# Diagonal score blocks on 32-row steps, a reversed key order for odd heads, and a new order of all queues in a two-kind attention kernel

## The chip, the cores and the metric

The kernel runs on one core of a Trainium2 chip. The metric is the device time of one execution in microseconds; the time before is the median of three runs, 480.24 us (479.35 to 480.51). A core has five instruction queues that run beside each other: TensorE (PE, with its weight loads shown as PEld), VectorE (DVE), ScalarE (ACT), GpSimd (POOL) and SyncE (SP, which issues most DMAs). Each queue runs in the order in which it was written; between queues only semaphores order the work.

## The reference

Four layers with a residual each, in the order A, B, A, B, on 2048 tokens of width 512 with 32 heads of 16. A is attention in four segments of 512 tokens with a running memory, B is linear attention with a softmax feature map. Both begin with a layer norm. Cut to what matters:

```python
# A, for segment s of 512 tokens
logits = einsum('bhqd,bhkd->bhqk', qs, ks) * 0.25 + mask     # mask: keys after the query are out
p = softmax(logits)
a_dot = einsum('bhqk,bhkd->bhqd', p, vs)
num, den = phi(qs) @ M, phi(qs) @ z + 1e-6                   # memory of the segments before
o = g * num / den + (1 - g) * a_dot
M, z = M + phi(ks)^T vs, z + sum(phi(ks))
# B, over all 2048 tokens
phi_k = [softmax(k w_phi), softmax(-k w_phi)];  phi_q likewise
o = phi_q @ (phi_k^T v) / (phi_q @ sum(phi_k) + 1e-6)
```

## The kernel before

**Stages.** `build` records about 3,100 operations for two layers; each layer is one A and one B. In A the core walks through four segments (`a_proj`, `a_att`, `a_state`, `a_mem`), and the key part of B (`b_keys`) for a segment's tokens and the query part (`b_queries`) are recorded between them. `b_out` of the first layer's chunks 1 to 3 is recorded among the second layer's A segments, so the second layer's attention has more PE work beside it.

**Scores.** `a_att` makes scores transposed: keys on the 128 partitions, queries along the row. A head has only 16 numbers, so a 32-row strip of PE holds two heads; the keys of the even head (`par` 0) and of the odd head (`par` 1) stand in two copies, each with zeros where the other head's rows are. Four strips `a` = 0 to 3 lie in the four 32-row groups of the array. One score operation `y` does strips 2y and 2y+1 into a pair of PSUM banks, 512 columns each; one ACT instruction then takes the exp of both banks at once (`128x1024`) into a tile PT. Where the order marks it, two score operations are issued interleaved, so that all four row groups work (a matmul list of 28 in place of 14).

**Diagonal blocks.** A unit with two diagonal blocks D and one full block S fills the 512 columns of a bank: 3 x 64 for each D and 128 for S. For one D, the even and the odd head share 192 columns of 128 rows: 64 columns hold the first 64 queries of both heads, over a stationary operand KP that has the first 64 keys of the even head in rows 0 to 63 and those of the odd head in rows 64 to 127; then 64 columns with the later 64 queries of each head. KP is copied together from K once per 128 tokens (L938 and L939), and the odd head's keys stand with their two halves of 64 swapped: `a_proj` makes a 64-column second copy of the normed input (`lo`, L907) so that a window of 128 columns over it reads the tokens in that order. The triangle is cut out after the exp by two kinds of masks: `mask.odd` (L1110) multiplies the odd heads' part by a 0/1 table `modd` into a tile D, in two instructions of 256 elements a row (either on DVE or on POOL), and `mask.even` (L1113), always on POOL, clears the even heads' part of PT in place with a select. The even mask waits for both odd masks of its tile, since they share columns. Then `pv` multiplies each 128 x 128 block of PT or D (as weights) by 17 columns of V.

**What sets the order.** Nothing is scheduled at build time. `replay` takes four tables: `ORDER` lists every operation by number (a number over 10000 is interleaved with the one before it; a negative one puts idle matmuls on the tile `warm` into PE's queue, L1431), `ENGINE` says which engine takes each operation that may run on several, `SLOTS` which buffer each tile gets, `AFTER` adds waits. All buffers, waits and queue positions follow from them.

Of the kernel before, what the change touches and what calls it, by code (L numbers as in the profile page):

```python
# [20 lines left out]
NG = 4  # L21
# [518 lines left out]
class Kernel:  # L540
# [299 lines left out]
    def xtiles(self, xnT):  # L840

        return xnT.ap if xnT.pool is self.p_xA else xnT.ap[:].rearrange("p t (d c) -> p t d c", d=4)
# [191 lines left out]
    def a_att(self, s, tss, seg, AM, starts, ends, done, by_pe=()):  # L1034
# [22 lines left out]
        for n, unit in enumerate(units):  # L1057
# [8 lines left out]
            if diag:  # L1066
                offs = [0, 4, 2]
# [408 lines left out]
```

## Time and profile before

The page of the profiled execution gives the span (first to last instruction), each engine's busy time, and where the chain of waits ran that ended last. Busy time of PE is modelled from pipelined matmuls and runs high.

| | before |
|---|---|
| median of three runs | 480.24 us |
| profiled execution, span | 479.8 us |
| instructions | 19249 |
| PE busy, by the trace | 464.4 us (97%), 8324 matmuls |
| ACT busy | 430.7 us (90%), 668 instructions |
| DVE busy | 428.1 us (89%), 1021 instructions |
| POOL busy | 261.0 us (54%), 420 instructions |
| first attention exp starts, last one ends | 12.8 us, 433.3 us |
| last exp of layer 0 ends, first of layer 1 starts | 203.4 us, 238.8 us |
| granted TensorE clock | 1.00 throughout |

The stages used below are read off the exps: 12.8 to 203.4 us is the attention of layer 0, 203.4 to 238.8 us the step between the layers, 238.8 to 433.3 us the attention of layer 1, and the rest is start and tail.

### The profile page before, as it was taken

The numbers are of one execution on the slowest core, as the hardware profiler recorded it, in microseconds if no ns is written. First come the engines' busy times: TensorE is split into PE (matmuls) and PEld (weight loads), VectorE is DVE, ScalarE is ACT, GpSimd is POOL, SyncE is SP. The second block draws the span as 40 slices with busy tenths as digits, with TensorE's granted clock in tenths as the row PEclk, the third lists the DMA queues.
The fourth block names the chain that finished last, engine by engine and source line by source line (L and its number), as shares of the span: only waits on it lengthen the run. The fifth ranks groups of instructions, "written<-read, shape, count | busy, mean of one in ns | idle before, by whom it ended". The sixth has DMA issues, their size and how long they took to land.

```text
span 479.8 us, 19249 instructions
## 1 busy us (share of the span) xinstructions
PE 464.4 (97%) x8324; PEld 320.1 (67%) x8324; DVE 428.1 (89%) x1021; ACT 430.7 (90%) x668; POOL 261.0 (54%) x420
## 2 busy tenths in 40 slices
PE   8999989999999999999999999999999999999997
PEld 7776667667856567557687666766865657665763
DVE  6999999989998988599999899999998879978785
ACT  3999999999999999986799899899999999999743
POOL 3577657646756576410246485784776578761100
PEclk9999999999999999999999999999999999999999
DMA  8978752225411232232257407236145112402376
GB/s 264 160 196 132 127 78 46 46 48 78 59 23 25 46 68 47 19 39 47 55 88 93 62 9 124 58 53 81 39 56 89 25 25 48 76 19 55 69 128 187
DMA packets 115091, 35.86 MB, mean 75 GB/s; under 512 B 106816, under 2 KB 115008, under 8 KB 115008
## 3 DMA queue, kind: packets, MB, share of 16 engines
q1 hardware_dynamic: 113184, 33.06, 39.9%
q10 hardware_dynamic: 1824, 1.58, 1.0%
q8 instruction: 65, 1.06, 0.9%
q14 instruction: 18, 0.15, 0.1%
HBM read 6.32 MB, written 2.10 MB: 18 GB/s over the span
## 4 chain that ended last, share of the span: by engine, by line
PE 40%; DVE 25%; ACT 22%; DMA 8%; POOL 3%; issue 1%; POOLq 0%; DVEq 0%
PE PS L520 38%; ACT PT L1104 16%; DVE stats L801 4%; DMA OT<-O 3%; ACT Ek L1200 3%; DVE xn L817 2%; DVE X L1165 2%; DMA EQ<-xn 2%; POOL PT L1113 2%; DVE Vt L1228 1%; DVE D L1110 1%; DMA xA<-xn 1%; DMA xB<-xn 1%; PE PS L1431 1%; DVE O L1139 1%
## 5 line engine op out<-in xcount | busy, mean ns | idle before, releaser
L1104 ACT ACTIVATE PT<-PS 128x1024 bf16<-128x1024 f32 x288 | 282.4, 1068 | 6.5 <-PE PS L520 5.6
L1110 POOL TENSOR_TENSOR D<-PT,modd 128x256 bf16<-128x256 bf16 x127 | 87.2, 697 | 41.7 <-ACT PT L1104 29.5
L1113 POOL TENSOR_SCALAR_AFFINE_SELECT PT<-PT 128x512 bf16<-128x512 bf16 x128 | 83.2, 658 | 48.1 <-DVE D L1110 43.3
L520 PEld LDWEIGHTS PS<-VT,PT 128*128 128x128 bf16 x2048 | 74.7, 96 | 18.7 <-POOL PT L1113 3.8
L520 PE MATMUL PS<-VT,PT 128*128 128x17 bf16 x2048 | 81.7, 171 | 1.5 <-POOL PT L1113 0.6
L520 PE MATMUL PS<-QT,K 32*128 32x64 bf16 (+2 forms) x2176 | 74.8, 213 | 1.1 <-ACT PT L1104 0.6
L520 PE MATMUL PS<-VT,D 128*128 128x17 bf16 x512 | 59.8, 170 | 0.0
L520 PEld LDWEIGHTS PS<-QT,K 32*128 32x128 bf16 x2176 | 40.4, 93 | 20.3 <-ACT PT L1104 10.0
L1110 DVE TENSOR_TENSOR D<-PT,modd 128x256 bf16<-128x256 bf16 x129 | 45.1, 364 | 2.1 <-ACT PT L1104 2.0
L520 PEld LDWEIGHTS PS<-VT,D 128*128 128x128 bf16 x512 | 43.2, 96 | 0.0
L1228 DVE TENSOR_TENSOR Vt<-PS,Zk 128x1024 bf16<-128x1024 f32 (+1 forms) x34 | 38.9, 1159 | 1.1 <-ACT Zk L1216 0.6
L801 DVE BATCH_NORM_STATS2 stats<-X 128x6 f32<-128x512 bf16 x56 | 37.6, 683 | 1.1 <-DMA X<-in_A_x_dram 0.7
L1200 ACT ACTIVATE Ek<-PS 128x512 bf16<-128x512 f32 x64 | 36.8, 648 | 1.6 <-PE PS L520 1.4
L1207 POOL TENSOR_TENSOR Vt<-Ek 128x512 f32<-128x512 bf16 x24 | 28.2, 1175 | 17.4 <-ACT Ek L1200 15.1
L520 PE MATMUL PS<-WA_k,xA 128*128 128x256 bf16 x256 | 36.6, 273 | 0.8 <-DVE xA L907 0.5
L1165 DVE TENSOR_TENSOR X<-X,PS 128x512 bf16<-128x512 bf16 x50 | 33.5, 678 | 4.3 <-PE PS L520 4.0
L1304 POOL COPY O<-rho 128x512 bf16<-128x512 bf16 x26 | 16.2, 642 | 38.7 <-DVE rho L1297 35.4
L520 PE MATMUL PS<-xA,WA_q 128*128 128x128 bf16 x512 | 36.4, 219 | 0.7 <-DMA xA<-xn 0.5
L520 PE MATMUL PS<-WA_v,xA 128*128 128x256 bf16 x256 | 36.3, 273 | 0.3 <-DMA xA<-xn 0.3
L520 PE MATMUL PS<-WA_o,OT 128*128 128x512 bf16 x128 | 32.1, 380 | 1.3 <-DMA OT<-O 0.7
L520 PEld LDWEIGHTS PS<-xA,WA_q 128*128 128x128 bf16 x512 | 30.0, 98 | 4.8 <-issue 1.0
L817 DVE TENSOR_SCALAR xn<-X,mv,rstd 128x512 bf16<-128x512 bf16 x64 | 28.6, 466 | 4.1 <-POOL rstd L813 1.7
(158 smaller groups left out, 983.5 us busy)
## 6 DMA issues: line engine op xcount, KB each, us to landing
X<-in_A_x_dram SPq DMA_DIRECT2D x3, 512.0 KB, 11.7
out_dram<-X SPq DMA_DIRECT2D x12, 128.0 KB, 1.8
EQ<-in_B_wqkv_dram SPq DMA_DIRECT2D x2, 512.0 KB, 4.9
OT<-O SPq DMA_TRANSPOSE x42, 3.2
WB_v<-in_B_wqkv_dram SPq DMA_DIRECT2D x1, 512.0 KB, 10.9
WA_o<-in_A_wo_dram SPq DMA_DIRECT2D x1, 512.0 KB, 4.1
WB_o<-in_B_wo_dram SPq DMA_DIRECT2D x1, 512.0 KB, 4.9
out_dram<-X ACTq DMA_DIRECT2D x4, 128.0 KB, 2.3
```

What stands on the lines that cost most here:

```text
L520: return e.matmul(o, l, r, start=st, stop=sp, tile_position=(basep(l), basep(o)))
L801: self.dve(lambda e, t=t, src=src: e.bn_stats(self.stats[:, t, :], src()), 0.603, [held() if held else R("X", t)], [R("stats", t)], name=" ...
L817: self.dve(lambda e, t=t, n=n, xn=xn: e.tensor_scalar(xn.ap[:, n], self.X[:, t, :], self.mv[:, t, 0:1], self.rstd[:, t:t + 1], op0=ALU.sub ...
L1104: self.act(lambda e, st=st, pt=pt: e.activation(pt.ap[:].rearrange("p b c -> p (b c)"), self.ps[:, st.slot[0] * 512:st.slot[0] * 512 + 102 ...
L1110: self.either(lambda e, d=d, k=k, pt=pt: e.tensor_tensor(d.ap[:, :, k, :].rearrange("p b (z c) -> p b z c", z=2), self.ends(pt.ap[:, :, 25 ...
L1113: self.pool(lambda e, q=quarters: e.affine_select(q(), q(), [[0, 4], [1, 128]], ALU.is_ge, 0.0, base=0, channel_multiplier=-1), 0.6, [pt() ...
L1139: self.dve(lambda e, r1=r1, view=view, nt=nt, g=g, o=o[ts]: e.tensor_tensor(o.ap[:, 0:nt, g, :].rearrange("p i (h d) -> p i h d", d=DH), v ...
L1165: self.dve(lambda e: e.tensor_tensor(X[:, t, :], X[:, t, :], self.bank(gen), ALU.add), 0.6, [R("X", t), gen()], [R("X", t)], name="resid")
L1200: self.act(lambda e, sgn=sgn, Ek=Ek, gen=gen: e.activation(Ek.ap[:, sgn, :], self.bank(gen), ACT.Exp, scale=1.0 - 2.0 * sgn), 512, [gen()] ...
L1207: self.pool(lambda e, Ek=Ek, sums=sums: e.tensor_tensor(sums(), *(Ek.ap[:].rearrange("p s (h j) -> p s h j", h=H)[:, :, :, 8 * k:8 * k + 8 ...
L1228: self.dve(lambda e, w=w, n=n, Vt=Vt, Zk=Zk, gen2=gen2: e.tensor_tensor(self.signed(Vt)[:, w, :, 0:16], self.bank(gen2).rearrange("p (h d) ...
L1304: P.add(("act", "pool"), {"act": lambda e, dst=dst, src=src: e.activation(dst(), src(), ACT.Copy), "pool": lambda e, dst=dst, src=src: e.t ...
```

## The change

A diagonal block takes 160 columns in place of 192, so a unit with two of them fills 448 of a bank's 512 columns and its exp runs over `128x896`. The odd head's keys now stand in fully reversed token order (key 127 - p in row p), so that the even head's triangle lies in the upper rows and the odd head's in the lower rows of shared columns. A block is made by five matmuls on each strip in place of three: even keys x queries 32 to 127 (96 columns); odd keys x queries 64 to 127 in reversed order (64 columns); odd keys, rows 64 to 127 only, x queries 32 to 63 (32 columns); odd keys, rows 96 to 127 only, x queries 0 to 31 (32 columns); even keys, rows 0 to 31 only, x queries 0 to 31 (32 columns). The last three write over parts that the masks would clear. KP and its copies are gone; `lo` now copies 128 reversed columns; for the tiles whose keys come straight from PSUM the odd copy is one instruction in place of two. `mask.odd` is one instruction over 512 elements a row that reads PT backwards: a multiplication on DVE or a select on POOL.

The two small odd blocks take their queries forwards, while the mask reads those columns backwards: for the first 64 queries of a diagonal tile the odd heads' scores are those of the query mirrored within its 32 columns. Amount and kind of work are the same as with the other direction.

```diff
-        self.p_xA = slots("xA", 2, [128, 4, 4, 192], BF16)
+        self.p_xA = slots("xA", 2, [128, 4, 4, 256], BF16)
-        self.p_KP = slots("KP", 4, [128, NG, 128], BF16)
...
+    def turn(self, a):
+        n = a.shape[-1]
+        return bass.AP(a.tensor, a.offset + n - 1, [list(x) for x in a.ap[:-1]] + [[-1, n]])
...
-            lo_d, lo_s = (lambda tt=tt: self.xcol(xnT, slice(None), tt, 128, 64)), (lambda tt=tt: self.xcol(xnT, slice(None), tt, 0, 64))
+            lo_d, lo_s = (lambda tt=tt: self.xcol(xnT, slice(None), tt, 128)), (lambda tt=tt: self.turn(self.xcol(xnT, slice(None), tt)))
...
-            op = P.add(("dve", "act", "pool"), {"dve": lambda e, d=kp_d, s=kp_s: e.tensor_copy(d(), s()), ...
-                       {"dve": 0.21, "act": 0.53, "pool": 0.58}, [K((0, tt)), K((1, tt)), K((1, tt, 1)), K(("both", tt))], [kp()], lat=0.08, name="kp")
...
+            cols = [(128, 0), (288, 160), (0, 320)] if diag else [(64 * off, 64 * off) for off in offs]
+            wide = 448 if diag else 512
...
-                        put(lambda a, g=g, i=i: both(a, g, i), item, i * 128, off, 64)
-                        for par in range(2):
-                            put(lambda a, par=par, g=g, i=i: strip(a, par, g, i), item, i * 128 + 64, 6 + off // 4 if par else off + 1, 64)
+                        keys = lambda par, lo, hi, g=g, i=i: lambda a: strip(a, par, g, i, lo, hi)
+                        put(keys(0, 0, 128), item, i * 128 + 32, x, 96, 64)
+                        put(keys(1, 0, 128), item, i * 128 + 64, x, 64, back=True)
+                        put(keys(1, 64, 128), item, i * 128 + 32, x, 32, 64, 64, 128)
+                        put(keys(1, 96, 128), item, i * 128, x, 32, 96, 96, 128)
+                        put(keys(0, 0, 32), item, i * 128, x, 32, 32, 0, 32)
...
-                    for k in range(2):
-                        self.either(lambda e, d=d, k=k, pt=pt: e.tensor_tensor(
-                            d.ap[:, :, k, :]..., self.ends(pt.ap[:, :, 256 * k:256 * k + 64], 384 - 192 * k), self.modd[:]..., ALU.mult), 0.21, 0.63, ..., name="mask.odd")
+                    op = P.add(("dve", "pool"), {"dve": lambda e, odd=odd, turned=turned: e.tensor_tensor(odd(), turned(), self.modd[:, None, :].to_broadcast([128, 4, 128]), ALU.mult),
+                                                 "pool": lambda e, odd=odd, turned=turned: e.affine_select(odd(), turned(), [[0, 4], [1, 128]], ALU.is_ge, 0.0, base=-127, channel_multiplier=1)},
+                               {"dve": 0.334, "pool": 0.59}, [pt(), pt("e"), R("modd")], [d()], lat=0.08, port=True, name="mask.odd")
```

All four tables are new; a line of `ORDER`, its first, was and is:

```diff
-    0, 20, 26, 1, 23, 21, 22, 2, 3, 24, 25, 28, 4, 5, 33, 81, 27, 6, 7, 82, 8, 9, 10, 11, 53, 16, 54, 18, 55, 60, 56, 17, 57, 12, 61, -401, 62, 63,
+    26, 0, 20, -323, 11, 2, 78, 8, 6, 4, 10, 5, 79, 21, 24, 1, 25, 27, 31, 30, 3, 22, 7, 14, 50, 9, 17, 51, 52, 32, 57, 13, 53, 18, 54, 58, 55, 59,
```

How many instructions of each kind there are, counted over the whole program (before, now): matmuls 8326 and 9230, among them idle ones on `warm` 144 and 24; exps over 1024 columns 288 and 160, over 896 columns 0 and 128; `mask.odd` on DVE 129 (256 elements a row) and 49 (512), on POOL 127 and 79; KP copies 32 and 0; stretches of score matmuls between other PE work 175 and 162, of which 85 and 76 hold a diagonal block. The stores of the result are split 12 on SP and 4 on ACT before, 8 and 8 now.

**First place: PE, the first interleaved pair of diagonal units (layer 0, segment 0).** Names: QT holds the queries, K the keys, KP the joined keys; the size is output rows x columns. Before:

```order
L520 MATMUL PS<-WA_v,xA0 128x256 x4
L1431 MATMUL PS<-warm 128x240 x2
L520 MATMUL PS<-QT0,KP0 128x64 x4
L520 MATMUL PS<-QT0,K0 128x64 x8
L520 MATMUL PS<-QT0,KP1 128x64 x4
L520 MATMUL PS<-QT0,K0 128x64 x8
L520 MATMUL PS<-QT0,K0 128x128 x4
```

and now, up to the first of the two diagonal blocks (the second follows with the same four rows, and then the 128 columns of the full block):

```order
L519 MATMUL PS<-WA_k,xA0 128x256 x4
L519 MATMUL PS<-QT1,K0 128x96 x4
L519 MATMUL PS<-QT1,K0 128x64 x4
L519 MATMUL PS<-QT1,K0 64x32 x4
L519 MATMUL PS<-QT1,K0 32x32 x8
```

The pair went from 28 to 44 matmuls, with outputs of 128, 64 and 32 rows one after the other, and the idle matmuls ahead of it are gone.

**Second place: POOL, the masks in layer 0.** PT holds exps, D the odd heads' masked part, `modd` the 0/1 table. Before:

```order
L1110 TENSOR_TENSOR D1<-PT4,modd 128x2x128
L1113 AFFINE_SELECT PT4<-PT4 128x4x128
L1110 TENSOR_TENSOR D2<-PT8,modd 128x2x128 x2
L1113 AFFINE_SELECT PT8<-PT8 128x4x128
L938 COPY KP2<-K1 128x2x4x64
```

and now:

```order
L1199 TENSOR_TENSOR Vt0<-Ek2 128x512
L1099 AFFINE_SELECT D2<-PT6 128x512
L1101 AFFINE_SELECT PT6<-PT6 128x4x128
L1099 AFFINE_SELECT D1<-PT8 128x512
L1101 AFFINE_SELECT PT8<-PT8 128x4x128
L1099 AFFINE_SELECT D3<-PT9 128x512
```

A tile's two odd masks became one select that stands just ahead of its even select on the same queue, and the KP copies between them are gone.

**Third place: PE at the start of segment 3 of layer 0.** Before:

```order
L520 MATMUL PS<-VT1,PT5 128x17
L520 MATMUL PS<-VT1,D2 128x17
L520 MATMUL PS<-QT1,K1 128x128 x16
L1431 MATMUL PS<-warm 128x240 x12
L520 MATMUL PS<-QT0,KP1 128x64 x4
L520 MATMUL PS<-QT0,K1 128x64 x8
```

and now:

```order
L519 MATMUL PS<-MSb1,PhiQ0 128x128 x8
L1423 MATMUL PS<-warm 128x240
L519 MATMUL PS<-QT2,K1 128x128 x2
L519 MATMUL PS<-QT1,K1 128x96 x2
L519 MATMUL PS<-QT2,K1 128x128 x2
L519 MATMUL PS<-QT1,K1 128x64 x2
L519 MATMUL PS<-QT2,K1 128x128 x2
L519 MATMUL PS<-QT1,K1 64x32 x2
L519 MATMUL PS<-QT2,K1 128x128 x2
L519 MATMUL PS<-QT1,K1 32x32 x4
```

The 12 idle matmuls that stood between two stretches of score work have gone, a plain unit is now interleaved with a diagonal one, and so 128-row, 64-row and 32-row outputs alternate.

More of the change, by code (lines that the diff above doesn't have):

```diff
@@ L713, in setup @@
         m = self.p_D.tile()
-        tri = lambda dst, src, base, step: pool(lambda e: e.affine_select(dst(), src(), [[step, 128]], ALU.is_ge, 0.0, base=base, channel_multiplier=1 if step == 0 else -1), 0.3, [m()], [m()])
-        m0, m1, m2 = (lambda: m.ap[:, 0, 0, :]), (lambda: m.ap[:, 0, 1, :]), (lambda: m.ap[:, 1, 0, :])
-        pool(lambda e: e.memset(m0(), 1.0), 0.2, (), [m()])
-        tri(m1, m0, 64, 1)
-        tri(m2, m1, -64, 0)
-        tri(m1, m0, -64, 1)
-        pool(lambda e: e.tensor_tensor(self.modd[:], m1(), m2(), ALU.add), 0.3, [m()], [R("modd")])
+        pool(lambda e: e.memset(m.ap[:, 0, 0, :], 1.0), 0.2, (), [m()])
+        pool(lambda e: e.affine_select(self.modd[:], m.ap[:, 0, 0, :], [[1, 128]], ALU.is_ge, 0.0, base=-127, channel_multiplier=1), 0.3, [m()], [R("modd")])
         for par in range(2):
@@ L894, in a_proj @@
         K, VT = self.p_K.tile(), self.p_VT.tile()
-        seg = dict(K=K, VT=VT, KP=[self.p_KP.tile() for _ in range(4)], QT=[self.p_QT.tile() for _ in range(2)])
+        seg = dict(K=K, VT=VT, QT=[self.p_QT.tile() for _ in range(2)])
         if s >= 1:
@@ L915, in a_proj @@
                 for par in range(2):
-                    for z in range(par + 1):
-                        cd = slice(tt * 128 + 64 * z, tt * 128 + (64 * z + 64 if par else 128))
-                        cs = slice(64 * (1 - z), 64 * (2 - z)) if par else slice(0, 128)
-                        dst = lambda par=par, cd=cd: K.ap[:, par, :, cd]
-                        src = lambda gen=gen, cs=cs: self.bank(gen).rearrange("p (g c) -> p g c", g=NG)[:, :, cs]
-                        P.add(("act", "dve"), {"act": lambda e, dst=dst, src=src, par=par: e.activation(dst(), src(), ACT.Copy, scale=self.even[:, par:par + 1]),
-                                               "dve": lambda e, dst=dst, src=src, par=par: e.tensor_scalar(dst(), src(), self.even[:, par:par + 1], None, op0=ALU.mult)},
-                              {"act": 0.36 if par else 0.57, "dve": 0.36 if par else 0.667}, [gen(), R("even", par)], [K((par, tt) if z == 0 else (par, tt, 1))], lat=0.1, name="kfm.copy")
+                    dst = lambda par=par, sl=sl: K.ap[:, par, :, sl]
+                    src = lambda gen=gen, par=par: (self.turn if par else lambda a: a)(self.bank(gen).rearrange("p (g c) -> p g c", g=NG))
+                    P.add(("act", "dve"), {"act": lambda e, dst=dst, src=src, par=par: e.activation(dst(), src(), ACT.Copy, scale=self.even[:, par:par + 1]),
+                                           "dve": lambda e, dst=dst, src=src, par=par: e.tensor_scalar(dst(), src(), self.even[:, par:par + 1], None, op0=ALU.mult)},
+                          {"act": 0.57, "dve": 0.667}, [gen(), R("even", par)], [K((par, tt))], lat=0.1, name="kfm.copy")
             else:
@@ L1075, in a_att @@
                     for c, i in enumerate(item[4]):
-                        where[item[1], item[2], item[3], i] = (pts, lambda d, b, x=(off + 2 * c) * 64: d[:, b, x:x + 128])
+                        where[item[1], item[2], item[3], i] = (pts, lambda d, b, x=(col[0] + 128 * c, wide + col[1] + 128 * c): self.flat(d)[:, x[b]:x[b] + 128])
             P.tag = (self.L, "att%d" % s)
@@ L1086, in f @@
                         def f(a=2 * y + b, b=b):
-                            x = st.slot[b] * 512 + c * 64
-                            return (self.ps[:, x:x + m], left(a), qt.ap[32 * a:32 * a + 32, item[1], q % 256:q % 256 + m], True, True)
+                            at = st.slot[b] * 512 + x[b] + dx
+                            qs = qt.ap[32 * a:32 * a + 32, item[1], q % 256:q % 256 + m]
+                            return (self.ps[lo:hi, at:at + m], left(a), self.turn(qs) if back else qs, True, True)
                         mms.append((f, m // 4))
-                for item, off in zip(unit, offs):
+                for item, x in zip(unit, cols):
                     g = item[1]
@@ L1093, in a_att @@
                         par, j, qs = item[2:]
-                        reads += [K((par, j)), K((par, j, 1)), K(("both", j))] + [QT[i // 2](i % 2) for i in qs]
-                        put(lambda a, par=par, g=g, j=j: strip(a, par, g, j), item, qs[0] * 128, off, 128 * len(qs))
+                        reads += [K((par, j)), K(("both", j))] + [QT[i // 2](i % 2) for i in qs]
+                        put(lambda a, par=par, g=g, j=j: strip(a, par, g, j), item, qs[0] * 128, x, 128 * len(qs))
                     else:
@@ L1102, in a_att @@
                 op = self.pe(mms, reads, [st()], pre=[pt], lat=0.23, cost=0.23, rows=y + 1, name="score")
                 op.place = (self.L, s, n)
[L1104 to L1105 removed]
+                self.act(lambda e, st=st, pt=pt, wide=wide: e.activation(
+                    self.flat(pt.ap)[:, 0:2 * wide].rearrange("p (b c) -> p b c", b=2), self.ps[:, st.slot[0] * 512:st.slot[0] * 512 + 1024].rearrange("p (b c) -> p b c", b=2)[:, :, 0:wide], ACT.Exp, scale=0.25), 2 * wide, [st()], [pt()], name="exp")
@@ L1106, in a_att @@
                 if diag:
                     d = ds[y]
-                    quarters = lambda pt=pt: pt.ap[:].rearrange("p b (k c) -> p (b k) c", k=2)[:, :, 0:128]
-                    for k in range(2):
-                        self.either(lambda e, d=d, k=k, pt=pt: e.tensor_tensor(
-                            d.ap[:, :, k, :].rearrange("p b (z c) -> p b z c", z=2), self.ends(pt.ap[:, :, 256 * k:256 * k + 64], 384 - 192 * k),
-                            self.modd[:].rearrange("p (z c) -> p z c", z=2)[:, None].to_broadcast([128, 2, 2, 64]), ALU.mult), 0.21, 0.63, [pt(), pt("e"), R("modd")], [d(k)], name="mask.odd")
+                    quarters = lambda pt=pt: self.every(self.flat(pt.ap)[:, 160:288], 160, 4)
@@ new lines, in a_att @@
+                    odd, turned = (lambda d=d: d.ap[:].rearrange("p b k c -> p (b k) c")), (lambda pt=pt: self.turn(self.every(self.flat(pt.ap)[:, 128:256], 160, 4)))
+                    op = P.add(("dve", "pool"), {"dve": lambda e, odd=odd, turned=turned: e.tensor_tensor(odd(), turned(), self.modd[:, None, :].to_broadcast([128, 4, 128]), ALU.mult),
+                                                 "pool": lambda e, odd=odd, turned=turned: e.affine_select(odd(), turned(), [[0, 4], [1, 128]], ALU.is_ge, 0.0, base=-127, channel_multiplier=1)},
+                               {"dve": 0.334, "pool": 0.59}, [pt(), pt("e"), R("modd")], [d()], lat=0.08, port=True, name="mask.odd")
@@ L1157, in a_att, with flat, every @@
                         done(i, oT, c)
-    def ends(self, a, step):
-        return bass.AP(a.tensor, a.offset, [list(a.ap[0]), list(a.ap[1]), [step, 2], [1, 64]])
+    def flat(self, a):
+        return a.rearrange("p b c -> p (b c)")
+    def every(self, a, step, n):
+        return bass.AP(a.tensor, a.offset, [list(x) for x in a.ap[:-1]] + [[step, n], list(a.ap[-1])])
     def residual(self, t, gen, X):
```

63 lines of the change are left out of this document (24 added, 39 removed), and 297 rows, old and new, of tables (AFTER, ORDER).

## The prediction

> **What bounds the kernel now.** I read the page's busy times and the chain that ended last first, then the windows by stage, then what PE waits for, then single rows of the groups and the timeline for durations.
>
> ```profile
> span 479.8 us, 19249 instructions
> ...
> PE 464.4 (97%) x8324; PEld 320.1 (67%) x8324; DVE 428.1 (89%) x1021; ACT 430.7 (90%) x668; POOL 261.0 (54%) x420
> ...
> PE 40%; DVE 25%; ACT 22%; DMA 8%; POOL 3%; issue 1%; POOLq 0%; DVEq 0%
> ...
> core 0: us, PE busy (x) PEld busy (x) DVE busy (x) ACT busy (x) POOL busy (x), PEclk, DMA share, GB/s
> ...
> 12.80:203.40 190.60, 184.88 (x3676) 128.15 (x3674) 175.10 (x434) 185.94 (x257) 121.09 (x190) 1.00 0.43 74
> 203.40:238.80 35.40, 35.02 (x403) 23.44 (x400) 32.84 (x66) 26.27 (x70) 5.04 (x8) 1.00 0.31 50
> 238.80:433.30 194.50, 190.31 (x3722) 132.24 (x3720) 177.55 (x434) 186.62 (x257) 126.86 (x196) 1.00 0.39 60
> 433.30:480.00 46.70, 43.02 (x424) 27.17 (x421) 33.55 (x61) 26.68 (x80) 3.27 (x6) 1.00 0.48 107
> ```
>
> No engine stands alone. In the two attention stages (first and third row of the stages, 385.1 of 480 us) ACT is busy 185.9 of 190.6 and 186.6 of 194.5 us, or 98% and 96%; DVE is at 92% and 91%; PE shows 97% and 98%, but its matmuls are pipelined and their ends modelled. What PE truly lacks is read from its waits, ahead of the weight loads, in the first and in the second attention stage (us in total, times, longest):
>
> ```profile
> PEld PS L520 <- ACT PT L1104: 12.5, 37, 0.6
> PEld PS L520 <- issue: 6.3, 26, 0.6
> ...
> PEld PS L520 <- issue: 9.0, 35, 0.5
> PEld PS L520 <- ACT PT L1104: 8.5, 26, 0.5
> ...
> q8 instruction: 65, 1.06, 0.9%
> ```
>
> The largest wait is for the exps: 12.5 + 8.5 = 21.0 us. A further 15.3 us has no releaser ("issue"), 61 times about 0.25 us; the last row counts 65 packets of instruction fetches, so I take these to be PE waiting for its next block of instructions. So ACT's exps bound the stages, with PE close behind; the second stage, with the other layer's output work beside it, is the tighter one for PE.
>
> **ACT.** 128 of the 288 exps shrink from 1024 to 896 columns.
>
> ```profile
> 142.67 8.44 ACT L1104 ACTIVATE PT<-PS 128x1024 bf16<-128x1024 f32 x9
> ...
> 411.34 3.17 ACT L1285 ACTIVATE EQ<-PS 128x512 bf16<-128x512 f32 x6
> ...
> L1104 ACT ACTIVATE PT<-PS 128x1024 bf16<-128x1024 f32 x288 | 282.4, 1068 | 6.5 <-PE PS L520 5.6
> ...
> L939 ACT ACTIVATE KP<-K 128x512 bf16<-128x512 bf16 x5 | 3.2, 637 | 0.0
> ```
>
> One exp shows 1.07 us from start to end, but nine in a row take 8.44: (8.44 - 1.07) / 8 = 0.92 us a step. Six of 512 columns step at about 0.50 us. That is 0.42 us for 512 columns, or 0.105 us for the 128 saved: 128 x 0.105 = 13.4 us. With the five KP copies (3.2 us) **ACT loses 16.6 us**, nearly all of it in the attention stages. The other moves on ACT (six evacuations of 512 columns fewer at 0.50 us, seven wider and four more small copies) cancel to about a microsecond and count as nothing. Four more stores are issued from ACT's queue, in the tail, where it is busy 26.7 of 46.7 us: no cost.
>
> **PE.** Three terms: wider blocks, fewer switches, more fetches.
>
> ```profile
> 146.01 0.38 PE L520 MATMUL PS<-VT,PT 128*128 128x17 bf16 x9
> ...
> 164.21 0.38 PE L520 MATMUL PS<-WA_o,OT 128*128 128x512 bf16 x1
> ...
> 164.43 1.03 PE L520 MATMUL PS<-EQ,WB_q 128*128 128x512 bf16 x4
> ...
> 166.11 0.17 PE L520 MATMUL PS<-VT,D 128*128 128x17 bf16 x1
> ...
> 166.21 0.40 PE L520 MATMUL PS<-QT,K 32*128 32x128 bf16 x16
> ...
> 166.55 1.40 PE L1431 MATMUL PS<-warm 128*128 128x240 bf16 x12
> ...
> 168.06 0.21 PE L520 MATMUL PS<-QT,KP 32*128 32x64 bf16 x4
> ...
> 168.40 0.96 PE L520 MATMUL PS<-H8b,K 128*128 128x8 bf16 x32
> ```
>
> A stretch of score matmuls holds 512 columns for each of the four row groups and takes 0.34 us to the next full-width matmul, whether it is 16 of 128 columns (166.21 to 166.55) or 28 mostly of 64 (168.06 to 168.40): the columns set it, not the count. Now a diagonal stretch holds 2 x (96 + 64 + 3 x 32) + 128 = 640. Columns pass at (1.03 - 0.38) / 3 / 512 = 0.42 ns (0.38 is a single one's length, in the row at 164.21), so 128 more are 0.054 us. The other end: no matmul of the trace steps below (0.38 - 0.17) / 8 = 26 ns, even with 17 columns; six 32-column ones at 26 in place of 13.4 ns add 0.076, together 0.13 us. Over 76 diagonal stretches that is 4.1 to 9.9 us. I take 9.9, since the 17-column row is the nearest in size. The switch itself: a score stretch starts 0.10 us after the last 17-column matmul, 0.07 more than the step, and its 0.34 us is 0.12 more than its 512 columns; so each stretch costs 0.19 us beside its work, and 13 fewer (175 to 162) save 2.5 us. 904 more matmuls with their loads are 1808 instructions; at 19249 / 65 = 296 a fetch that is six more, 1.5 us. **PE: +9 us** (low end +3). The 120 idle matmuls that go stood in waits, 12 of them in the 1.4 us row above, and count as nothing; without them PE idles there, and the granted clock, 1.00 in every row, would show it if that mattered.
>
> All new narrow matmuls change the shape of the array's output from 128 to 64 to 32 rows, within a stretch. No row of the trace shows that. The nearest is the switch between full width and 32-row groups, about 0.1 us each way; the other end is nothing, as between 64 and 128 columns above. These ends are 0 and 76 x 6 x 0.1 = 46 us, far apart. I take nothing: within a score stretch the row groups stay as they are, and the measured switch is one between row groups. The other end is rival 2.
>
> The Trainium skill speaks against me here: "TensorEngine Tiling (Array Packing)", section Key Properties, lists 32x128, 32x64 and 32x32 as different modes and says that a change of mode, not of tile alone, drains TensorE. By that rule rival 2 comes true; the trace agrees as far as it goes, since the row switch does cost 0.1 us. The same page says under Restrictions that column tiling disables the fast weight load; "TensorE: Matmul & The Clock Gate" has columns / 1.2 ns for a plain load, 53 ns for 64 columns, which by an estimate from that page would add two times 27 ns a stretch, 4 us in all; no run here shows it.
>
> **DVE and POOL.**
>
> ```profile
> L1110 POOL TENSOR_TENSOR D<-PT,modd 128x256 bf16<-128x256 bf16 x127 | 87.2, 697 | 41.7 <-ACT PT L1104 29.5 <-PE PS L520 4.9 <-DVE PhiQ L961 2.4
> L1113 POOL TENSOR_SCALAR_AFFINE_SELECT PT<-PT 128x512 bf16<-128x512 bf16 x128 | 83.2, 658 | 48.1 <-DVE D L1110 43.3 <-DVE VT L737 0.7 <-DVE Vt L1221 0.5
> ...
> L1110 DVE TENSOR_TENSOR D<-PT,modd 128x256 bf16<-128x256 bf16 x129 | 45.1, 364 | 2.1 <-ACT PT L1104 2.0
> ...
> L950 DVE TENSOR_TENSOR PhiK<-PhiK,phi 128x512 bf16<-128x512 bf16 x20 | 9.0, 450 | 0.9 <-ACT phi L948 0.8
> ...
> L1165 DVE TENSOR_TENSOR X<-X,PS 128x512 bf16<-128x512 bf16 x50 | 33.5, 678 | 4.3 <-PE PS L520 4.0
> ...
> L1149 POOL TENSOR_TENSOR O<-O,AM 128x512 bf16<-128x512 bf16 x1 | 1.4, 1393 | 0.8 <-DVE O L1139 0.8
> ...
> L938 POOL COPY KP<-K 128x512 bf16<-128x512 bf16 x14 | 8.6, 614 | 2.1 <-DMA K<-ktok 1.5 <-DVE K L922 0.6
> ...
> L938 DVE COPY KP<-K 128x512 bf16<-128x512 bf16 x13 | 4.1, 316 | 0.2 <-PE PS L520 0.2
> ...
> DVE xn L817 <- POOL rstd L813: 1.7, 4, 0.7
> ...
> PEld PS L520 <- POOL PT L1113: 3.8, 11, 0.6
> ```
>
> On DVE 45.1 us of odd masks become 49 of 512 elements. Reading backwards is not in the trace; the bounds are 0.45 (a bf16 product of that size) and 0.68 us (a sum that reads PSUM): 22 to 33 us, and I take 22, since operation and types are the first row's. With KP (-4.1) and six more evacuations from PSUM at 0.68 (+4.1), DVE gets 12 to 23 us shorter. On POOL 87.2 us become 79 selects between 0.66 (the even select) and 1.39 us (the slowest 512-element product): 52 to 110, KP takes 8.6 off, so 217 to 275 of 480 us. I take 52, by the same instruction. The waits that the even select had for DVE (43.3 us) turn into its place behind the odd select on POOL's own queue; behind the pair stand the powers of the layer norm, for which DVE waits 1.7 us in all, and the masked tiles, for which PE waits 3.8. Neither engine bounds, so all this counts as nothing; at the dear end those two waits could double, 5 us.
>
> **The sum.** PE's 21.0 us of waiting for exps shrink by what ACT loses, 16.6; PE's own work grows by 9: 479.8 - 16.6 + 9 = 472.2 us of span. The median of the runs stands 0.4 above the profiled span, so 472.6.
>
> **Rivals.**
> 1. *Half the relief arrives.* The exps get shorter, but PE, with 9 us more to do, is then late itself, above all in the second attention stage, where only 8.5 us were waits for exps and DVE is at 91%. If half of ACT's 16.6 us reaches the end: 479.8 - 8.3 + 9 = 480.5, with the 0.4 about 481. For it: the chain runs 40% through PE and 22% through ACT. Against it: the waits for exps exceed the whole saving.
> 2. *The shape changes drain PE (slower).* Six changes in each of 76 diagonal stretches at 0.1 us make 46 us; with the 9 and after all 21.0 us of waiting are used up: 479.8 + 46 + 9 - 21 = 514. It decides from 7.6 / 456 = 17 ns a change, where the gain is gone. For it: the row switch's price. Against it: stretches of 64 and 128 columns show no such step, and rows keep their groups.
> 3. *Cheap matmuls.* If 32 columns cost only their columns, PE grows by 3 us, and the sum is 466.6; a new order that also hides some of the 15.3 us of fetch waits in other waits takes a few more, about 464.
>
> That the change does less than it says is no case: the order holds the 128 narrow exps and no KP.
>
> **How the numbers follow.** Forecast (467 to 478) 0.48; rival 1 (478 to 487) 0.22; rival 2 (over 495) 0.16; rival 3 (459 to 467) 0.14. The likeliest gives 472.6. The range 461 to 487 leaves out rival 2 and a tail of rival 3, 0.20 together. Faster by over 0.3% (below 478.8; less can't be told from no change): 0.48 + 0.14 + 0.04 of rival 1 = 0.66; within 0.3%: 0.10; slower: 0.08 of rival 1 and rival 2 = 0.24.
>
> **What would show it.** Right: exps of 896 columns stepping at about 0.81 us, PE's waits on exps down from 21.0 to under 10 us, paired diagonal stretches at 0.40 to 0.47 us to the next full-width matmul, odd selects at 0.66 us. Wrong: a paired stretch near 0.9 us (rival 2); waits on exps unchanged; odd masks that run twice as long and PE waiting for POOL; or a granted clock below 1.00 where idle matmuls went.

## The result, and the profile after

The changed kernel takes **532.64 us** (531.26 to 535.97) against 480.38 us (479.35 to 480.65) for the kernel before on the same chip: 1.110 times the time, 95% interval 1.105 to 1.114. It is 52 us slower; 472.6 was predicted.

The page of the changed kernel, in the same rows as before: span, busy times, granted clock by slices, the chain.

```profile
span 534.2 us, 20823 instructions
...
PE 511.7 (96%) x9159; PEld 358.3 (67%) x9228; DVE 406.9 (76%) x932; ACT 424.8 (80%) x661; POOL 216.6 (41%) x349
...
PEclk9989989999999958999999999979996999799999
...
q8 instruction: 73, 1.20, 0.9%
...
PE 79%; ACT 9%; DVE 6%; DMA 2%; issue 2%; POOL 1%; SPq 0%; DVEq 0%; POOLq 0%
```

ACT, DVE and POOL all do less than before, and PE's share of the chain has gone from 40% to 79%: PE alone now sets the end. The granted clock, 1.00 in every stage before, has dips. The windows by stage (columns as in the prediction's: PE, PEld, DVE, ACT, POOL, granted clock, DMA share, GB/s; the bounds are again the first and the last exp of each layer):

```profile
0.00:17.10 17.10, 12.21 (x114) 9.90 (x115) 9.80 (x34) 5.61 (x10) 3.84 (x16) 1.00 0.89 277
17.10:231.60 214.50, 208.34 (x4118) 147.57 (x4143) 161.15 (x386) 181.37 (x251) 102.72 (x159) 0.94 0.33 59
231.60:265.90 34.30, 33.35 (x389) 22.84 (x394) 30.61 (x64) 28.51 (x75) 4.18 (x7) 1.00 0.29 55
265.90:487.70 221.80, 217.57 (x4152) 153.86 (x4184) 171.41 (x394) 182.62 (x251) 101.36 (x159) 0.95 0.30 54
487.70:534.20 46.50, 40.18 (x396) 24.18 (x397) 33.91 (x60) 26.66 (x80) 4.46 (x8) 1.00 0.45 103
```

The loss lies in the two attention stages: 190.6 to 214.5 and 194.5 to 221.8 us, together 51 us. ACT, which filled 98% and 96% of them, fills 85% and 82%. The head grew by 4.3 us as well. What the engines wait for in the whole execution (us in total, times, longest):

```profile
ACT PT L1092 <- PE PS L519: 59.8, 86, 2.7
...
PEld PS L519 <- issue: 26.6, 100, 0.8
...
PEld PS L519 <- ACT PT L1092: 12.4, 41, 0.4
```

The exps now wait 59.8 us for scores (5.6 before), PE waits less for exps than before (12.4 in place of 21.0 us). The reason stands in PE's timeline, at the first paired diagonal stretch (44 score matmuls) and the full-width matmuls around it:

```profile
18.71 0.38 PE L519 MATMUL PS<-WA_k,xA 128*128 128x256 bf16 x2
19.03 1.16 PE L519 MATMUL PS<-QT,K 32*128 32x96 bf16 x44
20.12 0.61 PE L519 MATMUL PS<-WA_k,xA 128*128 128x256 bf16 x4
```

From 19.03 to 20.12 are 1.09 us, where 0.40 to 0.47 was expected and 0.34 stood before. 47 paired stretches have this length in the median, and the 14 single ones of 22 matmuls 1.03 us. Score stretches without small blocks are as before (0.33 us). Narrower windows of the same timeline begin with the first matmul of each shape in this stretch:

```profile
19.03 0.22 PE L519 MATMUL PS<-QT,K 32*128 32x96 bf16 x4
...
19.21 0.33 PE L519 MATMUL PS<-QT,K 32*64 32x32 bf16 x8
...
19.35 0.36 PE L519 MATMUL PS<-QT,K 32*32 32x32 bf16 x12
```

At each of the six changes 0.12 to 0.13 us lie between the start of the last matmul of one shape and the first of the next. The eight matmuls of 32 rows write to two different places of the output, rows 96 to 127 and rows 0 to 31, and start 3 to 4 ns apart: the place makes no step, the shape does. Two stretches of 44 matmuls change shape 12 times and take 1.90 us.

### The profile page after: what moved, and what is told of

Same layout as the page of the kernel before. It is cut to its first block, busy times and chain, and to the rows that moved or that the text cites. A ratio compares the mean times of both kernels' runs of the same rounds, so it can differ in the third digit from the quotient of the medians.

```text
span 534.2 us, 20823 instructions
## 1 busy us (share of the span) xinstructions
PE 511.7 (96%) x9159; PEld 358.3 (67%) x9228; DVE 406.9 (76%) x932; ACT 424.8 (80%) x661; POOL 216.6 (41%) x349
## 3 DMA queue, kind: packets, MB, share of 16 engines
q1 hardware_dynamic: 112608, 32.54, 32.2%
## 4 chain that ended last, share of the span: by engine, by line
PE 79%; ACT 9%; DVE 6%; DMA 2%; issue 2%; POOL 1%; SPq 0%; DVEq 0%; POOLq 0%
PE PS L519 78%; ACT PT L1092 5%; DVE Vt L1220 1%; DMA X<-in_A_x_dram 1%; PE PS L600 1%; ACT Ek L1192 1%; DMA xA<-xn 1%; DVE O L1334 1%; DVE stats L794 1%; DVE KV L1249 1%; ACT K L1277 1%; DVE Rkv L1251 1%; DVE X L1157 0%; POOL PT L1101 0%; DVE Zk L1203 0%
## 5 line engine op out<-in xcount | busy, mean ns | idle before, releaser
L1092 ACT ACTIVATE PT<-PS 128x1024 bf16<-128x1024 f32 (+1 forms) x288 | 268.1, 983 | 60.8 <-PE PS L519 59.8
L519 PE MATMUL PS<-QT,K 32*128 32x128 bf16 (+5 forms) x3712 | 134.2, 211 | 0.8 <-ACT K L1277 0.3
L519 PEld LDWEIGHTS PS<-QT,K 32*128 32x128 bf16 (+2 forms) x3712 | 79.4, 93 | 52.0 <-ACT PT L1092 9.9
L1099 POOL TENSOR_SCALAR_AFFINE_SELECT D<-PT 128x512 bf16<-128x512 bf16 x79 | 51.0, 649 | 90.0 <-ACT PT L1092 45.0
L1192 ACT ACTIVATE Ek<-PS 128x512 bf16<-128x512 f32 x64 | 35.2, 611 | 3.8 <-PE PS L519 3.5
L519 PEld LDWEIGHTS PS<-xA,WA_q 128*128 128x128 bf16 x512 | 32.2, 102 | 3.8 <-issue 1.6
L1126 DVE RECIPROCAL r<-PS 128x16 f32<-128x16 f32 (+1 forms) x72 | 17.1, 240 | 23.0 <-PE PS L519 22.6
L519 PE MATMUL PS<-WA_o,OT 128*128 128x512 bf16 x108 | 29.6, 389 | 2.3 <-issue 1.0
L519 PE MATMUL PS<-WB_o,OT 128*128 128x512 bf16 x117 | 29.5, 379 | 1.0 <-issue 0.3
L519 PEld LDWEIGHTS PS<-WA_v,xA 128*128 128x128 bf16 x256 | 23.7, 100 | 8.3 <-ACT QT L578 2.3
```

The lines of the kernel that those rows point to most:

```text
L519: return e.matmul(o, l, r, start=st, stop=sp, tile_position=(basep(l), basep(o)))
L1092: self.act(lambda e, st=st, pt=pt, wide=wide: e.activation(self.flat(pt.ap)[:, 0:2 * wide].rearrange("p (b c) -> p b c", b=2), self.ps[:, ...
L1099: "pool": lambda e, odd=odd, turned=turned: e.affine_select(odd(), turned(), [[0, 4], [1, 128]], ALU.is_ge, 0.0, base=-127, channel_multip ...
L1126: self.dve(lambda e, r1=r1, view=view, nt=nt: e.reciprocal(r1.ap[:, 0:nt, :], view()[:, :, :, 16]), 0.07 + 0.0475 * nt, [pv()], [r1()], na ...
L1192: self.act(lambda e, sgn=sgn, Ek=Ek, gen=gen: e.activation(Ek.ap[:, sgn, :], self.bank(gen), ACT.Exp, scale=1.0 - 2.0 * sgn), 512, [gen()] ...
```

## The experiments

Theory A: each change of the output's rows (128, 64, 32) inside a stretch drains PE. Theory B: it is the number and the size of the matmuls. Theory C: the idle matmuls that went had held up the clock. The recorded expectations call the kernels by their labels: e1_wide has no shape change, e2_group two changes a stretch and e3_one one; e8_wide_first, e5_wide_loads and e9_wide_early are e1_wide with other orders of the loads, e6_one_loads and e10_one_early likewise e3_one, e7_loads and e11_early the changed kernel.

### No shape change

Each small block is made over all 128 keys and writes over its neighbours' scores, so that every matmul has one shape. This kernel leaves out the right scores of those neighbours:

```diff
-                        put(keys(1, 64, 128), item, i * 128 + 32, x, 32, 64, 64, 128)
-                        put(keys(1, 96, 128), item, i * 128, x, 32, 96, 96, 128)
-                        put(keys(0, 0, 32), item, i * 128, x, 32, 32, 0, 32)
+                        put(keys(1, 0, 128), item, i * 128 + 32, x, 32, 64)
+                        put(keys(1, 0, 128), item, i * 128, x, 32, 96)
+                        put(keys(0, 0, 128), item, i * 128, x, 32, 32)
```

> The changed kernel with the three narrow matmuls of each diagonal block made with all 128 keys, so that every score matmul has 128 output rows; number, columns and order of the matmuls stay. The narrow blocks then write over neighbouring scores. Theory A (a change of the output's shape inside a score stretch costs about 0.11 us, six of them in a diagonal stretch; the lower clock follows from that): a paired diagonal stretch falls from 1.09 to 0.40-0.47 us, the granted clock is 1.00 again, and the time is 465-480 us. Theory B (904 more small matmuls cost by their number or their width): the stretch and the time stay, 525-535 us. Theory C (the new order, with few idle matmuls, loses the clock): the stretch falls, but the clock stays near 0.95 and the time near 490-500 us.

Measured: **479.32 us**, 0.9985 of before (0.9972 to 0.9998). 53 us come back with the same number of matmuls and the same columns. PE's timeline of this kernel, at the same stretch:

```profile
17.34 0.49 PE L519 MATMUL PS<-WA_k,xA 128*128 128x256 bf16 x3
17.76 0.55 PE L519 MATMUL PS<-QT,K 32*128 32x96 bf16 x44
18.25 0.61 PE L519 MATMUL PS<-WA_k,xA 128*128 128x256 bf16 x4
```

17.76 to 18.25 is 0.49 us in place of 1.09. The 0.60 us between them over six changes are **0.10 us a change**; the same steps start to start are 0.01 to 0.02 us here. Theory B falls: number and columns are the same. Theory C falls as the main cause: the few idle matmuls are the same, and the granted clock is 0.98, not 1.00 as theory A had it. What this run leaves open is whether the narrow matmuls are slow by themselves and not by the change; the next two keep them narrow and only sort them.

### Fewer shape changes

The matmuls of a stretch are sorted by shape, in a pair over both halves, so two changes are left:

```diff
+                    for w in (128, 64, 32):
+                        one, two = by_shape(op.mms, w), by_shape(beside.mms, w)
+                        for k in range(0, max(len(one), len(two)), 2):
+                            for f in one[k:k + 2] + two[k:k + 2]:
...
```

> The changed kernel with the matmuls of a score stretch sorted by shape: all with 128 output rows, then 64, then 32; an interleaved pair ends with one semaphore step of two. Two changes of shape inside a diagonal stretch in place of six. Theory A: 76 stretches x 4 changes x 0.11 us = 33 us less, 495-503 us, less if the clock recovers; a paired diagonal stretch takes 0.6-0.7 us. Theory B: 525-535 us, as the same matmuls are issued. Theory C: 525-535 us.

Measured: 489.0 us, 1.0195 (1.0175 to 1.0214). Then the block of 64 rows is made by two of 32 rows, which leaves one change and adds eight matmuls to a pair:

```diff
-                        put(keys(1, 64, 128), item, i * 128 + 32, x, 32, 64, 64, 128)
+                        put(keys(1, 64, 96), item, i * 128 + 32, x, 32, 64, 64, 96)
+                        put(keys(1, 96, 128), item, i * 128 + 32, x, 32, 64, 96, 128)
```

> As the sorted kernel, but the block with 64 output rows is made by two matmuls of 32 rows: one change of shape inside a diagonal stretch, and two more matmuls a block for each bank pair. Theory A: 76 x 5 x 0.11 = 42 us less than the changed kernel, 485-495 us or less, and faster than the sorted kernel; a paired diagonal stretch takes 0.5-0.6 us. Theory B: slower than the sorted kernel, over 530 us, with 512 more matmuls. Theory C: no change, 525-535 us.

Measured: 483.0 us, 1.0067 (1.0040 to 1.0094). The timelines of the two kernels at that stretch, first with two changes, then with one:

```profile
18.59 0.72 PE L523 MATMUL PS<-QT,K 32*128 32x96 bf16 x44
19.24 0.61 PE L523 MATMUL PS<-WA_k,xA 128*128 128x256 bf16 x4
```

```profile
18.54 0.61 PE L523 MATMUL PS<-QT,K 32*128 32x96 bf16 x52
19.08 0.61 PE L523 MATMUL PS<-WA_k,xA 128*128 128x256 bf16 x4
```

1.09, 0.65, 0.54 and 0.49 us for six, two, one and no change, and 532.6, 489.0, 483.0 and 479.3 us of time: both fall with the changes, at 0.05 to 0.10 us each in the stretch. So narrow matmuls alone are not slow, and theory A is shown. Both times lie below the ranges of theory A (495 to 503 and 485 to 495), which left room for a clock that recovers: the mean granted clock of the runs is 0.95 to 0.96 with six changes and 0.985 to 0.996 with two or one. In the sorted traces too a change is 0.11 to 0.14 us from the last start to the first; the stretch grows by less because the sorted narrow matmuls follow each other more closely (32 of them start within 0.12 us in e3_one, where 24 take 0.15 us in e1_wide).

### The idle matmuls, taken from the kernel before

```diff
         for n, x in enumerate(ORDER):
+            if x < 0 and n > 64:
+                continue
```

> The kernel before without its 119 idle matmuls after the first 25. Theory A: they stood in waits and the array is busy enough without them; 478-482 us, clock 1.00. Theory C (idle matmuls hold the clock): granted clock below 0.98 and the time over 488 us.

Measured: 485.0 us, 1.0120 (1.0074 to 1.0166). The page's row of the granted clock, and one stretch of this kernel and of before:

```profile
PEclk9999999999999959999999999999997998999999
```

```profile
169.00:180.20 11.20, 10.38 (x204) 6.09 (x189) 7.62 (x25) 8.98 (x13) 7.70 (x12) 0.54 0.37 72
```

```profile
169.00:180.20 11.20, 10.87 (x199) 6.51 (x196) 9.63 (x26) 10.59 (x16) 8.51 (x13) 1.00 0.39 73
```

In the same 11 us PE now runs at 0.54 of its clock, and ACT and DVE get less done. So the idle matmuls were worth 5 us in the order of before, between the two answers (478 to 482, over 488). That is a tenth of the loss; theory C has a part at most.

### The loads at the start

With theory A settled, 479.3 is still 6.7 us above the prediction's sum. The kernel without shape change has two holes in PE, 3.4 us at 5.2 us and 3.0 us at 26.5 us. PE's timeline around the second:

```profile
25.47 1.06 PE L519 MATMUL PS<-xA,WA_q 128*128 128x128 bf16 x16
29.59 1.01 PE L519 MATMUL PS<-WA_v,xA 128*128 128x256 bf16 x4 [3.05 <-DMA xA<-xn]
```

PE waits for transposed tokens, and before that, in the head, for the tile X1, which the new `ORDER` puts behind 512 KB of other tokens on SP's queue (in its first line, 11 stands ahead of 1). Theory H: the first loads are all of it. Rival T: transposes that are issued behind large loads. First only the first loads go back to their order of before:

```diff
+def loads_first(order):
+    moved = {1, 2, 3, 4, 5, 6, 7, 8, 9, 10, 11}
+    behind = {-323: (1, 2, 3, 4, 5, 6, 7, 8, 9, 10, 11)}
+    return [y for x in order if x not in moved for y in (x,) + behind.get(x, ())]
...
-        for n, x in enumerate(ORDER):
+        for n, x in enumerate(loads_first(ORDER)):
```

> The kernel of e1_wide (no shape change) in which only the first loads are put back in the order of before: the tiles X0 to X3 and the weights WA_k, WA_q, WA_v alternately on the two load queues, and the 512 KB of X rows behind them; e1_wide issues those 512 KB first on SP's queue, and PE then idles 3.4 us from 5.2 us on, with the first exp at 16.4 us against 12.8 before. Theory H (the order of the first loads costs the head, and that is all): PE's gap at 5 us goes, the first exp comes at about 13 us, and the end comes 3.4 us earlier, at about 476. Rival T (the loads that are issued next hold up the token transposes on SP's queue, and that decides): the gap of 3 us at 26.5 us, in which PE waits for xA, stays or grows by what the head gains, and the time stays within a microsecond of 479.3.

Measured: 480.3 us, 0.9991 (0.9975 to 1.0007). The first exp comes 2.5 us earlier, at 13.95, and nothing of it reaches the end; the waits of this kernel between 20 and 32 us say why:

```profile
PE PS L529 <- DMA xA<-xn: 6.7, 1, 6.7
```

The hole at 26.5 us, 3.0 us long, has become one of 6.7 us from 24.1 us on. H falls. Then the loads that follow go to about their places of before as well (13 and 14 are the raw query and key weights, 512 KB each, 15 and 19 WA_o and WB_o, 397, 398 and 407 transposes of the raw weights):

```diff
-    behind = {-323: (1, 2, 3, 4, 5, 6, 7, 8, 9, 10, 11)}
+    behind = {-323: (1, 2, 3, 4, 5, 6, 7, 8, 9, 10, 11, 16, 17, 18, 12), 318: (14, 13), 132: (15, 397, 398), 332: (407,), 425: (19,)}
...
```

> e8_wide_first, and in addition the other loads and the transposes of the raw weights are put back to about the places of before: WB_v and the X rows right behind the first loads, the raw query and key weights behind three transposes of xn, WA_o and the transposes of the raw weights behind the next ones of the keys, WB_o later. Theory H: no more than e8_wide_first, about 476. Theory T: both gaps of PE (3.4 us at 5 us and 3.0 us at 26.5 us) go, and with them the half clock that follows them (3.4 and 6.8 us in e1_wide, worth up to 5 us): 479.3 - 6.4 - 0 to 5 = 468 to 473, which is where the prediction's sum stood without the shape changes (472.6).

Measured: 477.9 us, 0.9942 (0.9926 to 0.9958), in neither range: short of what T gave (468 to 473) and of H's 476. The hole had moved:

```profile
34.52 0.72 PE L529 MATMUL PS<-QT,K 32*128 32x96 bf16 x44 [4.13 <-DMA K<-ktok]
```

The keys' transpose was issued at 27.4 us, right behind the megabyte of raw weights at 25.7 us. (In the kernel before, the same megabyte is issued at 22.0 and the keys' transpose at 26.6 us, and PE has no such hole.) In the same order the kernel with one change, with the two small odd blocks read backwards too:

> The kernel of e3_one (matmuls sorted by shape, one change a stretch) with the load order of e5_wide_loads; the two small odd blocks read their queries backwards, as the large one does. e3_one has the same two gaps (3.3 us at 5.2, 2.6 us at 27.5). Theory T: 483.0 - 5.9 - 0 to 3 = 474 to 477, faster than before (479.7). Theory H: about 479.7. If reading backwards in small blocks costs PE anything, the paired stretch rises above 0.54 us.

Measured: 479.2 us, 0.9982 (0.9966 to 0.9997), not the 474 to 477 of T, with the same hole (3.5 us at 30.2 us). The stretch stayed at 0.54 us, so reading small blocks backwards costs PE nothing. And the changed kernel itself with these loads:

> The changed kernel with the load order of e5_wide_loads and nothing else altered, shape changes and all. If the loads are a term of their own, the time falls by what e5_wide_loads gains on e1_wide, or by the two gaps at least (3.3 and 2.0 us): 532.6 - 5 to 11 = 521 to 528. If the drained PE hides them (the head's loads arrive in time for a slower PE), it falls by 3.4 at most: 529 to 533.

Measured: 529.3 us, 1.1037 (1.0989 to 1.1085). That is in the second range, but its runs (526.2 to 533.3) reach into both, so this does not tell them apart. The step to the kernel without shape change is 51.4 us here.

Last, the raw weights go right behind the first loads (the DMA share in the run before was 0.10 and 0.07 between 16 and 20 us):

```diff
-    ... 11, 16, 17, 18, 12), 318: (14, 13), 132: (15, 397, 398), 332: (407,), 425: (19,)}
+    ... 11, 16, 17, 18, 12, 14, 13), 132: (397, 398), 332: (407, 15), 425: (19,)}
```

> e5_wide_loads (no shape change, loads about as before) with the raw query and key weights (1 MB) loaded right behind the first loads, while the transfers idle from 16 us on, and WA_o behind the transposes of the raw weights. In e5_wide_loads PE still stood 4.0 us at 30.4 us, waiting for transposed keys whose transfer was issued at 27.4 us right behind that megabyte, and half the clock followed from 34.3 us for 3.4 us. Theory T (a transpose that is issued behind a large load waits for it, and PE with it): the gap goes, the first attention stage shrinks by 4 us and up to 1.7 more for the clock, 477.9 - 4 to 5.7 = 472 to 474. Rival (the first stage is bound by something else, and PE would wait elsewhere): the gap goes but the last exp of the first layer still comes 205 to 206 us after the start, and the time stays at 477 to 478.

Measured: **471.9 us**, 0.9835 (0.9818 to 0.9853). Its windows by stage (head, attention of layer 0, the step between, attention of layer 1, tail) and the waits that it still has:

```profile
0.00:12.90 12.90, 9.94 (x115) 8.06 (x116) 9.34 (x31) 5.55 (x11) 3.82 (x16) 1.00 0.85 265
12.90:198.30 185.40, 177.21 (x4118) 129.94 (x4142) 159.90 (x388) 177.92 (x251) 103.29 (x159) 0.99 0.41 75
198.30:232.60 34.30, 33.36 (x389) 22.84 (x394) 30.63 (x64) 28.50 (x75) 4.16 (x7) 1.00 0.29 55
232.60:422.30 189.70, 183.79 (x4158) 135.44 (x4190) 169.61 (x394) 179.42 (x252) 100.61 (x159) 1.00 0.37 63
422.30:468.60 46.30, 40.02 (x390) 24.04 (x391) 33.74 (x60) 26.55 (x79) 4.46 (x8) 1.00 0.46 104
```

```profile
PEld PS L529 <- issue: 17.7, 63, 1.3
PEld PS L529 <- ACT PT L1102: 14.8, 48, 0.5
```

No hole of over 1.2 us is left in PE, the last exp of layer 0 comes at 198.3 us, ACT fills 96% and 95% of the attention stages, and the clock is whole but for 3.4 us. The rival falls and theory T holds for this hole. The same order with one change a stretch:

> The same load order in e6_one_loads (one shape change a stretch, sorted), where PE stood 3.4 us at 30.2 us and half the clock followed for 6.8 us. Theory T: 479.2 - 3.4 - 0 to 3.4 = 472.5 to 476, faster than before (480.1) by 1 to 1.5%. Rival: 478 to 479.

Measured: **474.0 us**, 0.9893 (0.9869 to 0.9916). Nothing is left out of the computation here, and it beats both kernels: 1.1% faster than before, 11% faster than the change. And with all six changes:

> The changed kernel, six shape changes a stretch and all, with the load order of e9_wide_early; it stands to e9_wide_early (471.9) as the changed kernel (532.6) stands to e1_wide (479.3). If the shape changes and the loads are two terms that add, the step is 53 us again and the loads are worth 7.4 us here too: 525. If the drained PE hides what the loads cost: 529 to 533, a step of 57 to 61 us. The second question is the clock: 51 us at half in the changed kernel, 3.4 us in e9_wide_early. If holes between PE's instructions cause it (loads, waits), it is gone here as well, below 10 us; if the drained stretches themselves do, it stays at 30 us or more.

Measured: 527.8 us, 1.0963 (1.0916 to 1.1010), between the two answers: the step to the kernel without shape change is 55.9 us. The mean granted clock is 0.955 to 0.964 in all but one of these runs, which makes 38 to 47 us at half; so the second answer, 30 us or more, is the one that came. Where the half clock falls is read from the changed kernel with the loads of before (529.3 us): 41 us of it, and between the head and the tail PE has two holes of over 0.6 us there, 1.8 us at 32.2 and 0.8 us at 70.4, each next to a stretch at half. The other stretches at half, 17.1 us from 182.5 us on and three more, 31 us in all, follow no hole of over 0.5 us. Holes between the instructions are not needed: a program with six changes a stretch goes with a lower clock without them.

## Why the prediction was wrong

**The step that failed** is the one on the narrow matmuls: "I take nothing: within a score stretch the row groups stay as they are, and the measured switch is one between row groups." The ends, 0 and 46 us, were drawn right, and the choice between them was wrong: a change of the output's shape costs 0.10 us although the row groups stay. The evidence held against rival 2, that stretches of 64 and 128 columns show no such step, is about the columns that stream through; the outputs there all have 128 rows, so it could not tell. The rule that the prediction weighed and did not follow, the Trainium skill's in "TensorEngine Tiling (Array Packing)", Key Properties, that a change of mode drains TensorE, holds here, at 0.10 us for each of six changes a stretch.

**Rival 2 came true and was too small**, 514 against 532.6. It let all 21.0 us of waiting for exps be used up; 12.4 us are still there in the changed kernel. And it left the clock and the loads out. Between the changed kernel and the one without shape change lie 53.3 us in the medians and 56 in the profiled executions. By 76 x 6 x 0.10, 46 of them stand in the stretches; the traces have a little more, 95.8 against 44.9 us for all diagonal stretches together; mixed ones change shape more often, and 501 changes are counted in all. Beside that, the clock stands at half for 51 us where it did so for 20, and waits without a releaser rise from 21.3 to 26.6 us; the runs do not split these two.

**The other terms** are read from the kernel without shape change and with early loads, 471.9 us against the sum of 472.6:
- *ACT.* Two exps of 896 columns in a row take 1.73 us and a single one 0.92 (the two rows of ACT's timeline below), so the step is 0.81 us, as worked out. ACT's busy time in the two attention stages falls from 372.6 to 357.3 us, by 15.2 (16.6 predicted); between the layers it grows by 2.2.

```profile
281.48 0.92 ACT L1102 ACTIVATE PT<-PS 128x896 bf16<-128x896 f32 x1
...
287.79 1.73 ACT L1102 ACTIVATE PT<-PS 128x896 bf16<-128x896 f32 x2
```

- *PE.* The paired stretch takes 0.49 us; 0.34 + 0.13 = 0.47 was worked out with the dear end of the range, which was the right one. Its reading "no matmul of the trace steps below" 26 ns is too wide, as score matmuls stand closer (28 in 0.34 us), but a set of four with 32 columns, one for each row group, does take 25 to 26 ns here. Eight more fetch packets came, not six.
- *What that makes.* The attention stages are 5.2 and 4.8 us shorter, the step between the layers 1.1 and the tail 0.2, the head 0.1 longer, 11.2 together between the two profiled executions. Of these this one is 1.6 us below its median (470.3 against 471.9); between the medians lie 8.2 us, and the sum had 7.6. But PE's waits on exps fell only from 21.0 to 14.8 us, not under 10: the sum agrees better than its parts, and so in part by luck.
- *DVE and POOL*, from the page of the changed kernel. The odd select takes 0.65 us (its group is the row below), POOL falls to 216.6 and DVE by 21.2 us (12 to 23 predicted). Neither bounds.

```profile
L1099 POOL TENSOR_SCALAR_AFFINE_SELECT D<-PT 128x512 bf16<-128x512 bf16 x79 | 51.0, 649 | 90.0 <-ACT PT L1092 45.0
```

**Two costs set at nothing were not nothing.** The idle matmuls "count as nothing" in the prediction; in the order of before they are worth 5 us, and the granted clock falls without them, the sign that was named. In the changed order with early loads, which has 24 of 144, the clock nearly holds without them (0.989 to 0.996 in the mean), so there the term is about right. And the new order of the loads was not a step of the prediction at all, though the diff's first line has it: 479.3 - 471.9 = 7.4 us without shape changes, 483.0 - 474.0 = 9.0 with one, about 5 with six.

So the parts of the change pull apart: the shape changes cost 53 us, the load order 7, and all the rest (narrower exps, new masks, the new order of the other work) gains some 8; no run divides that gain.

**Open:** whether a stretch with shape changes lowers the clock in the same way as idle time does, whether the matmul's shape or that of its weight load, which changes with it, makes the step, and why the idle matmuls matter more in the old order than in the new one. No run tells.

## What to carry to other kernels

Work that is packed in pieces of several output shapes pays for the changes between the shapes, not for the pieces: sort by shape before counting matmuls, and where the price of an unseen operation has ends as far apart as the whole change, the forecast is a bet on that row. When a table reorders all queues, read the load queue first: a transpose that PE waits for soon should not be issued right behind a large load, and a load moved to the front can simply move the hole (the head gained 2.5 us, and the hole grew by 3.7). An unexplained hole in a profile is worth an experiment of its own even when the main cause is found.

## What the runs showed of the hardware

- At a change among outputs of 128, 64 and 32 rows, in the same 32-row groups, 0.11 to 0.14 us lie between the start of the last matmul of one shape and the first of the next. A stretch grows by about 0.10 us a change when shapes alternate, and by 0.05 to 0.08 us when they are sorted. Matmuls of 32 and 96 columns in one shape follow each other without such a step.
- The granted clock falls to half for 3.4 us or multiples of it (up to 17.1 us). Some of these stretches begin in or shortly after a hole of 1.0 to 6.7 us in PE. Others follow no hole of over 0.5 us: most of those with six shape changes a stretch, and one at about 400 us in four of the kernels with none or one (479.3, 480.3, 477.9 and 479.2 us). In the 471.9 us kernel a hole of 1.2 us at 61.4 us goes with half the clock, and one of 1.0 us at 36.9 us does not.
- With 1 to 1.5 MB of loads issued shortly before on the same queue, a transpose that PE needs came so late that PE stood for 3.0 to 6.7 us in four of the kernels. With the raw weights issued at 10.7 us in place of 25.7 the last of these holes was gone.
